# The first k and v loads of an attention and expert kernel: one GpSimd queue in order of use, instead of v beside k on the SyncE queue

## The chip, the cores and the metric

The kernel runs on one core of a Trainium2 chip. The metric is the time of one execution on the device, in microseconds (us); each kernel was run several times and the median is quoted, with the lowest and highest run. A run counts as slow here when it is over 1.5% above the fastest of its kernel; all runs were fast but two of one kernel near the end, which are left out there. A second kind of number comes from the trace of one profiled execution: times within it are counted from the start of its span, which is some 2 us shorter than the device time.

Four chips took part. The kernel before takes 315.7 us on the first, 320.5 on the second and third and 316.8 on the fourth (medians), so kernels are compared only with runs of the kernel before on the same chip. TensorE, VectorE, ScalarE, GpSimd and SyncE appear in the trace as PE (its weight loads as PEld), DVE, ACT, POOL and SP; a `q` after the name (SPq) is an engine's queue of issued transfers.

## The reference

```python
def phi(x):                                   # x is q or k, scaled by D ** -0.25
    h = einsum('bhsd,md->bhsm', x, omega) - sum(x * x, -1, keepdims=True) / 2
    return exp(h - max(h, -1, keepdims=True)) / sqrt(m)
q_p, k_p = phi(q_s), phi(k_s)
kv  = einsum('bhsm,bhsd->bhmd', k_p, v)
z   = sum(k_p, axis=2)
out = einsum('bhsm,bhmd->bhsd', q_p, kv) / (einsum('bhsm,bhm->bhs', q_p, z) + 1e-6)
# ... out becomes the tokens of a mixture of experts: one expert per token by argmax,
# or the expert of the token before where a local gate says so; relu(x @ w1[e]) @ w2[e] times p[e]
```

B = 8, H = 8, S = 576, head size 64, 128 features; 8 experts, 512 to 1024 to 512. Only the first steps matter here: k is projected by omega, the row maxima of the projection are taken, and exp(projection) is multiplied with v.

## The kernel before

The attention part works through 36 units of k (9 for each P = 0 to 3). Each runs through a chain: transposes on TensorE, a copy `kt` on VectorE, projections by `om_bd` on TensorE, row maxima `kmx` on VectorE, exponentials `kp` and `ek` on ScalarE, and `va` (v times ek) on GpSimd, which TensorE then multiplies with `kp`. The loads:

```python
def load(P, nm, g):
    # ... a tile for q, k or v: 8 rows of 9 * 64 for q, 4 for k and v; 1152 KB for q and v, 576 KB for k
    # k has 4 buffers (bf16, converted by the DMA), v has 3 (float32)
    cuts = [0, 4, 9] if (P, nm, g) == (0, "k", 0) else [0, 9]
    for c0, c1 in zip(cuts, cuts[1:]):
        c = slice(c0 * Dh, c1 * Dh)
        (nc.sync if nm == "v" else nc.gpsimd).dma_start(out=t_[:, :, c], in_=rows[nm][:, j0:j0 + nj, c])

load(0, "k", 0)
# ... om_f (omega) and wgf (gate weights) loaded from ScalarE
load(0, "v", 0)
load(0, "k", 1)
load(0, "v", 1)
```

Calls of one engine keep their order; calls of different engines don't wait for one another. "k0a" and "k0b" are below the two pieces of the first k tile (4 and 5 of 9 columns), "k1" the second k tile, "v0" and "v1" the v tiles of P = 0, and "v2" the first v tile of P = 1. What stands between the loads and the chain are some constants:

```python
make_identity(nc, ident)                       # GpSimd
# ... ident_bf, om2 on VectorE
nc.tensor.transpose(t_ps, om2.rearrange("p a d -> p (a d)"), ident_bf)
om_t2 = consts.tile([128, M], BF)
nc.vector.tensor_copy(om_t2, t_ps)             # from PSUM
nc.vector.memset(om_bd, 0.0)
nc.vector.tensor_copy(om_bd[0:64, 0:M], om_t2[0:64])      # from SBUF: called "the om_bd copy" below
nc.vector.tensor_copy(om_bd[64:128, M:], om_t2[64:128])
```

And the schedule of the later loads, by iteration of the main loop:

```python
at(-1, load, 1, "k", 0)
at(-1, load, 0, "q", 0)
for P in range(1, NP):
    # ...
    at(max(9 * P - 9, 2), load, P, "v", 0)
    at(9 * P - 10, load, P, "k", 1)
    at(9 * P - 4, load, P, "v", 1)
    at(9 * P + LAG - 11, load, P, "q", 0)
```

From about 130 us on the second part runs: "pages" of gathered tokens go through the experts, 38 of them, with TensorE full from about 160 us.

## Time and profile before

| | before |
|---|---|
| device time, median of 3 (lowest to highest) | 315.73 us (315.63 to 315.75) |
| span of the profiled run, and its own device time | 318.8 us, 320.79 us |
| mean granted TensorE clock of that run | 0.959 |
| DMA traffic | 60.22 MB in 51562 packets |
| row maxima of units 0, 1, 2, 3 start at | 15.36, 18.13, 19.60, 21.15 us |
| first transposes of q, first gather of tokens | 32.61, 135.31 us |

Note the second row: the run that was profiled took 5 us longer than the three that were timed. Its early part can be read by itself, but its whole span is no partner for another kernel's span. The lines that carry the reading are in the prediction. Three more of this trace are wanted below as landmarks; the first number is the start, the second the duration, and brackets hold the idle time ahead with what ended it:

```profile
21.15 1.22 DVE L200 TENSOR_REDUCE kmx<-pj 128x8 f32<-128x1024 f32 x1
...
32.61 0.41 PE L171 MATMUL tp<-ident_bf,arena 128*64 128x128 bf16 x8
...
135.31 1.09 POOL L574 DMA_INDIRECT xg<-x_tok,ix  x1 [5.45 <-DVE pe L508]
```

They mark the end of the start-up (unit 3's row maxima), the arrival of q in the chain, and the hand-over to the experts. An early gain is worth something only if it is still there at the third.

### The profile page before, as it was taken

The page shows a single profiled execution, that of the slowest core. Times are in us where ns is not written, and L with a number is a line of the kernel's source. Part 1 is how long each engine was busy: PE and PEld are TensorE (multiplying, and loading weights), DVE is VectorE, ACT ScalarE, POOL GpSimd, SP SyncE. Part 2 cuts the span into 40 slices and gives each one's busy share as a digit, 9 for nine tenths or more (in the row PEclk, how much of TensorE's full clock was granted, in tenths as well). Part 3 has the DMA queues.
Part 4 walks back from the last instruction along what each step waited for, and adds up shares of the span by engine and source line. Part 5 has one row for each costly group of instructions (what it writes and reads, how often), then busy time and mean ns, then how long its engine had stood idle before and what let it go on. Part 6 is the DMA issues. An engine that isn't in the chain of part 4 may idle for free. (4 is left out here: it accounts for less than half of the span.)

```text
span 318.8 us, 8136 instructions
## 1 busy us (share of the span) xinstructions
PE 257.5 (81%) x2977; PEld 153.7 (48%) x2977; DVE 179.9 (56%) x406; ACT 151.0 (47%) x228; POOL 175.1 (55%) x264
## 2 busy tenths in 40 slices
PE   0266778787877775737989989999999999999991
PEld 0154555565555653523656556644444444444440
DVE  3487578979879868953555674333333331433440
ACT  1057698988989877514455445512222121222000
POOL 8459845755477743186585632145536556533452
PEclk9999899999999979756999999999999999999998
DMA  7999999999979999969999953247656695842222
GB/s 246 291 208 262 293 210 283 248 238 241 288 128 222 228 237 226 227 178 199 196 216 223 226 129 72 51 120 192 173 143 159 171 179 138 168 143 94 103 118 88
DMA packets 51562, 60.22 MB, mean 189 GB/s; under 512 B 24464, under 2 KB 33680, under 8 KB 51520
## 3 DMA queue, kind: packets, MB, share of 16 engines
q0 software_dynamic: 23088, 40.58, 60.3%
q1 hardware_dynamic: 24352, 14.29, 17.0%
q10 hardware_dynamic: 4080, 4.77, 4.6%
q8 instruction: 28, 0.46, 0.6%
q14 instruction: 14, 0.11, 0.1%
HBM read 67.16 MB, written 14.68 MB: 257 GB/s over the span
## 5 line engine op out<-in xcount | busy, mean ns | idle before, releaser
L604 PE MATMUL pj<-w_all,xt 128*128 x304 | 76.4, 385 | 3.6 <-DVE lt L294 3.4
L609 ACT ACTIVATE arena<-pj 128x1024 bf16<-128x1024 f32 x38 | 38.9, 1023 | 75.5 <-PE pj L604 58.1
L635 POOL DMA_INDIRECT out_dram<-y,idr x38 | 37.8, 995 | 53.1 <-DVE y L634 39.0
L218 POOL TENSOR_TENSOR va<-vs,ek 128x512 bf16<-128x512 f32 (+1 forms) x40 | 38.1, 956 | 34.5 <-ACT ek L209 34.3
L574 POOL DMA_INDIRECT xg<-x_tok,ix x36 | 37.4, 1038 | 30.7 <-PE tp L587 12.5
L200 DVE TENSOR_REDUCE kmx<-pj 128x8 f32<-128x1024 f32 x36 | 44.0, 1221 | 13.5 <-ACT kvb L237 8.6
L206 ACT ACTIVATE kp<-pj 128x1024 bf16<-128x1024 f32 x36 | 37.4, 1040 | 18.9 <-DVE kmx L200 18.9
L143 POOL DMA_DIRECT2D w_all<-in_moe_w_dram x64 | 35.8, 564 | 16.7 <-DMA w_all<-in_moe_w_dram 11.8
L604 PEld LDWEIGHTS <-xt 128*128 128x128 bf16 x304 | 28.9, 99 | 31.8 <-ACT xt L589 3.0
L267 ACT ACTIVATE qp<-pj 128x1024 bf16<-128x1024 f32 x36 | 37.6, 1045 | 11.1 <-PE pj L261 5.9
L634 DVE TENSOR_SCALAR y<-po,prb 128x512 f32<-128x512 f32 x24 | 18.0, 751 | 34.0 <-PE po L629 19.6
L194 PE MATMUL pj<-om_bd,kt 128*128 128x256 bf16 x144 | 23.5, 288 | 2.9 <-ACT kp L206 1.3
L168 PE MATMUL tp<-ident_bf,ks 128*128 128x128 bf16 x128 | 13.3, 230 | 15.4 <-DMA ks<-in_k_dram 7.6
L291 DVE TENSOR_TENSOR xr<-po,rd 128x512 bf16<-128x512 f32 x36 | 24.9, 691 | 1.2
L619 DVE COPY ht<-tp 128x1024 bf16<-128x1024 bf16 (+1 forms) x20 | 12.2, 608 | 22.5 <-PE tp L616 18.6
L629 PE MATMUL po<-w_all,ht 128*128 x104 | 24.6, 379 | 0.2 <-DVE y L634 0.2
L589 ACT COPY xt<-tp 128x512 bf16<-128x512 bf16 x19 | 11.1, 584 | 25.3 <-PE tp L587 22.0
L629 PEld LDWEIGHTS <-ht 128*128 128x128 bf16 x160 | 15.2, 98 | 16.3 <-issue 0.3
L619 DVE COPY arena<-tp 128x512 bf16<-128x512 bf16 (+1 forms) x18 | 9.2, 513 | 24.5 <-PE tp L616 12.1
L716 ACT COPY qt<-tp 128x512 bf16<-128x512 bf16 x36 | 21.8, 605 | 1.2 <-DVE kt L714 1.0
L629 PE MATMUL po<-w_all,arena 128*128 x88 | 20.8, 379 | 1.6 <-DVE y L634 1.6
L629 PEld LDWEIGHTS <-arena 128*128 128x128 bf16 x144 | 13.8, 98 | 16.6 <-issue 1.7
(154 smaller groups left out, 374.9 us busy)
## 6 DMA issues: line engine op xcount, KB each, us to landing
w_all<-in_moe_w_dram POOLq DMA_DIRECT2D x64, 256.0 KB
vs<-in_v_dram SPq DMA_DIRECT2D x8, 1152.0 KB
arena<-in_q_dram POOLq DMA_DIRECT2D x4, 1152.0 KB
x_tok<-xr ACTq DMA_DIRECT2D x16, 256.0 KB
ks<-in_k_dram POOLq DMA_DIRECT2D x7, 576.0 KB
out_dram<-y,idr POOLq DMA_INDIRECT x38
xg<-x_tok,ix POOLq DMA_INDIRECT x36
x_tok<-xr ACTq DMA_DIRECT2D x4, 128.0 KB
```

The costliest lines, as they stand in the source:

```text
L143: nc.gpsimd.dma_start(out=wdst[l][:, ds(e * WE + i * 1024, 1024)].rearrange("p (c f) -> p c f", f=w), in_=src[e].rearrange(("(c p) f -> p ...
L194: nc.tensor.matmul(pj[:, 2 * i:2 * i + 2, :].rearrange("p a d -> p (a d)"), lhsT=kts[t][:, i], rhs=om_bd, start=True, stop=True)
L200: nc.vector.tensor_reduce(mx, kpj[t], axis=AX, op=Alu.max)
L206: nc.scalar.activation(kp, kpj.pop(t), Act.Exp, scale=scale)
L218: nc.gpsimd.tensor_tensor(va[:, x:x + 4 * n, 0:Dh].rearrange("p (h r) d -> p h r d", h=4), stg[P, "v", g].rearrange("p h (r d) -> p h r d" ...
L267: nc.scalar.activation(qp, qpj.pop(s), Act.Exp, scale=scale)
L291: nc.vector.tensor_tensor(xrs[s][:, u % 2, :].rearrange("p (g h d) -> p g h d", g=2, h=4), ov[:, :, :, 0:Dh], rd.to_broadcast([128, 2, 4, ...
L574: nc.gpsimd.indirect_dma_start(out=xg, out_offset=None, in_=src, in_offset=bass.IndirectOffsetOnAxis(ap=ix, axis=0), bounds_check=TE - 1, ...
L604: nc.tensor.matmul(h_ps[:, c, :], lhsT=xt[:, dc, :], rhs=w1_all[:, ds(ev + (dc * F + c * 512), 512)], start=(dc == 0), stop=(dc == DC - 1))
L609: nc.scalar.activation(h, h_ps.rearrange("p a x -> p (a x)").rearrange("p (c f) -> p f c", f=FC), Act.Relu)
L629: nc.tensor.matmul(y_ps[:, 0, :], lhsT=htn[0][:, f], rhs=w2_all[:, ds(ev + f * D, D)], start=(f == 0), stop=(f == FC - 1))
L635: s_ = nc.gpsimd.indirect_dma_start(out=out_flat, out_offset=bass.IndirectOffsetOnAxis(ap=idr[:, c:c + 1], axis=0), in_=y, in_offset=None, ...
```

## The change

Intent: k is what the chain needs first, yet v's large packets take turns with it. With the first k and v in one queue, in order of use, nothing should go ahead of the first k.

```diff
-            (nc.sync if nm == "v" else nc.gpsimd).dma_start(...)
+            (nc.sync if nm == "v" and P else nc.gpsimd).dma_start(...)
...
-    load(0, "k", 0)
+    for nm_, g_ in (("k", 0), ("v", 0), ("k", 1), ("v", 1)):
+        load(0, nm_, g_)
 # ... om_f, wgf from ScalarE as before
-    load(0, "v", 0)
-    load(0, "k", 1)
-    load(0, "v", 1)
```

From line 114 on, lines of the changed kernel have numbers lower by 2 (L200 becomes L198).

> **What bounds the kernel now.** The chain of work that ended last is of no use here: it holds two pieces at 313 us, 0.3% of the span. So I read in this order: the slices of the page, busy time by stage, the waits of the first 20 us against those after them, and then the first 20 us instruction by instruction. The slices:
>
> ```profile
> PE   0266778787877775737989989999999999999991
> DMA  7999999999979999969999953247656695842222
> ```
>
> A slice is 8 us. TensorE does nothing in the first and little in the second, while the DMA engines are at 90% or more from the second slice on. Three stages follow: a head in which compute waits for data, the attention part up to about 112 us with no engine full, and an expert part in which TensorE is full. Busy time by stage:
>
> ```profile
> core 0: us, PE busy (x) PEld busy (x) DVE busy (x) ACT busy (x) POOL busy (x), PEclk, DMA share, GB/s
> 0.00:17.00 17.00, 2.70 (x17) 1.75 (x18) 7.08 (x9) 1.67 (x2) 10.35 (x28) 1.00 0.98 265
> 17.00:112.00 95.00, 74.61 (x1543) 53.59 (x1540) 78.41 (x145) 81.26 (x142) 63.50 (x119) 0.98 1.10 238
> 112.00:160.00 48.00, 33.52 (x524) 22.18 (x523) 31.04 (x106) 24.20 (x37) 24.45 (x35) 0.79 1.00 211
> 160.00:220.00 60.00, 56.68 (x431) 33.26 (x429) 30.16 (x91) 27.48 (x34) 29.02 (x37) 1.00 0.69 151
> 220.00:313.00 93.00, 90.00 (x472) 42.88 (x470) 33.26 (x55) 16.37 (x16) 46.95 (x48) 1.00 0.56 147
> ```
>
> From 17 us on, ScalarE (81 of 95) and VectorE (78 of 95) alternate on a chain, and from 160 us TensorE sets the pace. Waits for a loaded tile lie in the head alone; over 20 to 112 us the longest wait for any DMA is 0.4 us, of a weight load's issue:
>
> ```profile
> PEld L168 <- DMA ks<-in_k_dram: 9.6, 2, 7.8
> PE tp L168 <- DMA ks<-in_k_dram: 7.6, 1, 7.6
> ...
> POOL w_all L143 <- DMA w_all<-in_moe_w_dram: 0.4, 1, 0.4
> ```
>
> So the change, which touches only loads of the head, can win only what the head loses. There, in order of time:
>
> ```profile
> 0.81 59.31 SPq L103 DMA_DIRECT2D vs<-in_v_dram  x7
> 1.35 2.49 POOL L103 DMA_DIRECT2D ks<-in_k_dram  x3 [0.84 <-POOLq L837]
> 5.60 4.07 DVE L130 COPY om_bd<-om_t 64x128 bf16<-64x128 bf16 x1
> 7.06 2.56 POOL L332 IOTA io<- 128x768 bf16 x1
> 12.76 0.61 PE L168 MATMUL tp<-ident_bf,ks 128*128 128x128 bf16 x4 [7.59 <-DMA ks<-in_k_dram]
> 16.63 0.61 PE L168 MATMUL tp<-ident_bf,ks 128*128 128x128 bf16 x4 [1.31 <-DVE kmx L200]
> 19.60 1.22 DVE L200 TENSOR_REDUCE kmx<-pj 128x8 f32<-128x1024 f32 x1
> ```
>
> Units 0 and 1 wait for the first piece of k until 12.76, unit 2 for the second until 16.63 (the weight load before it names that DMA, 1.79 us). VectorE's row maxima come at 15.36, 18.13, 19.60 and 21.15; from the third on they follow at about 1.5 us. Why k is late, in the queues from 6 to 15 us:
>
> ```profile
> q1 hardware_dynamic: 1004, 2.26, 71.2%
> q0 software_dynamic: 913, 0.51, 39.3%
> q10 hardware_dynamic: 965, 0.02, 6.2%
> ```
>
> q0 is GpSimd's queue (k and q), q1 SyncE's (v), q10 ScalarE's. They send nearly the same number of packets, so they take turns, but v's packets have 2304 bytes and k's here 512 or 640. SyncE has three v loads queued at once (v has three buffers), the third of which, P = 1, is used only some 30 us later.
>
> **What the Trainium skill says.** "DMA: Bandwidth & Descriptors", section "Queues, rings and completion order", says that each DMA engine goes round robin over the queues that have work, a packet at a time; the equal counts above agree. The same page, "Issuing engines are not separate DMA queues", says that the issuing engine does not choose other DMA engines: moving v between queues changes order and not bandwidth. The trace agrees: the engines stay full from 3 to 30 us whatever queue is sending. "SBUF — State Buffer", section "Who interferes with whom", says that VectorE's copies in a two-port mode and GpSimd exclude each other, and the later one blocks entirely. The trace agrees: the L130 copy lasts 4.07 us, its twin L131 0.20, and it ends at 9.67, just after GpSimd's IOTA (9.62). "TensorE: Matmul & The Clock Gate", "What's actually happening", says that TensorE is at half rate until a window of about 3.4 us was busy; here four projections take 1.06 us up to 19.4 and 0.60 from 20.46.
>
> **The change part by part.** *Order of the queues.* Before: SyncE v0, v1, v2 (v2 is the first v of P = 1), GpSimd k0a, k0b, k1, k2, q0, k3. The order of instructions after: GpSimd k0a, k0b, v0, k1, v1, then the constants, then k2, q0, k3; SyncE has six v loads left, and its first, v2, now goes out at once, at 0.81. It finds the engines empty, as GpSimd's first packet came only at 6.0 (issue 1.35, so 4.7 us later). v2 thus takes the place of v0, 2.2 to about 6, and costs k nothing; v1 alone moves behind k1, v0 behind k0b.
>
> *When data land.* One load is 512 packets. Alone, v sends 350 packets in the 2 us from 3.75, so 512 take 2.9 us. 1152-byte packets (2397 in 13 us, 16 to 29) take 2.8 us a load. A 512-byte packet takes 59 ns in the trace and a 640-byte one 67, so over 16 engines k0a is 1.9 us and k0b 2.1, with 0.3 us each for ScalarE's small packets in turn. Summed from 6.0, with 0.3 for v2's tail: k0a sent by 8.5, k0b 10.9, v0 13.8, k1 16.6, v1 19.5, k2 22.3, q0 28.0, k3 30.8. Add 0.6 to 0.9 for the slowest engine and the signal (k1 in before: first of the 16 signals at 18.5, last at 19.4). k0a lands near 9.2 instead of 12.7, k0b at 11.6 instead of 16.6, k1 near 17.2 instead of 19.4.
>
> *What is added.* Two more issues on GpSimd ahead of the identity: 2 x 0.8 (2.49 for three) = 1.6 us. The identity, IOTA and the rest move by that: IOTA ends at 11.3. If the om_bd copy stays blocked until then, both om_bd copies end at 11.5, and only then comes the first kt copy (13.40 in before). So k's first 3.5 us are not all used: 13.40 - 11.5 = 1.9 us for unit 0.
>
> *The chain from there*, with durations of before, TensorE cold: kt0 11.5 to 11.9; second transposes 12.0; projections of unit 0 12.4 to 13.4; row maxima 0 13.45 to 14.7 (1.23), kt2 to 15.1, row maxima 1 15.1 to 16.3, kt3 to 16.75, row maxima 2 16.85 to 18.1, kt4, row maxima 3 18.5. In before that last one began at 21.15. Gain: 21.15 - 18.5 = 2.6 us. From the second gate: the transposes of unit 4 need k1, near 17.2; they are followed by the projections of unit 3 (0.6 + 0.6), and maxima 3 at 18.5 again. Both gates give the same 2.6, which is why I trust it. v0 lands at 14.5, its first use (after 16) is later.
>
> *What carries on.* k2 is needed near 26, lands at 23; q0 lands near 28.8, needed at 32.61 - 2.6 = 30.0; v1 lands at 20.3, needed near 23.5. Later loads have 8 us or more of slack by their landing times. The DMA engines must also follow 2.6 us earlier. They are full for most of 2 to 138 us, but have free time at 88 to 96 (share 0.77, 131 GB/s) and a little at 60 to 66; I estimate 4 to 5 us of it, more than 2.6. So the first gather, at 135.31 now, which waits for VectorE there, should move too, and the TensorE-bound rest with it. I take off 0.2 for small collisions: 315.73 - 2.4 = 313.3.
>
> **The rivals.**
> (1) The om_bd copy is the new gate and is blocked even longer by the extra GpSimd work: one more us lost, gain 1.5, about 314.2. For it: the 4.07 us. Against: it ended with IOTA, and the same list of work follows it.
> (2) q0 or k1 are late: the v load of P = 1, second half, goes out on SyncE 2.6 us earlier and takes turns with q0. Then iteration 9 stalls by 1 to 1.5 us: about 314.5. Against: in before that v load was issued at 27 and sent almost nothing until GpSimd's backlog ended at 29.75.
> (3) All is hidden: the weight loads fill the DMA engines, so the expert part begins when it did, 315.7. For it: GpSimd's weight loads at 112 to 130 wait for earlier ones, 0.4 to 1.4 us each. Against: the free time before 96 us, and that the gathers then wait 5.45 us for VectorE, not for a DMA.
> (4) The clock: TensorE has half its clock in several windows of 3.4 us between 115 and 150 (mean 0.79 from 112 to 160). One window more or fewer is up to 1.7 us of full-rate work, in either direction. I cannot predict it.
> (5) A larger gain: om_bd is not blocked, and k0b at 11.6 is the gate. But k1 caps it: again about 2.6.
>
> **Range and chances.** The middle is 313.3. Rivals 1 to 3 make it 314 to 315.7, a clock window fewer 311.6, so 311.5 to 315.9 holds 8 times in 10. Over 2% would be 309.4 or 322.0: the whole gap from 9.9 to 12.76 and the second stall together are not 6.3 us, so faster is 0.03; slower needs a large new stall, 0.02; within 2% is 0.95.
>
> **What would show it.** First transposes of k near 9.3 and not 12.76, but the first kt copy only near 11.5, with a long om_bd copy before it ending with IOTA; row maxima 3 near 18.5; no wait of GpSimd's va products for v; the first transposes of q near 30; first gather near 132.7. Queue q1 holding one v load in the first 15 us. It would be wrong if the first gather is still at 135 (rival 3), if the transposes of q wait for the DMA (rival 2), or if the head gains 2.6 and the end shows something else with another mean clock (rival 4).

## The result, and the profile after

| | before | after |
|---|---|---|
| median (lowest to highest), 4 runs each, alternating on one chip | 315.74 us (315.63 to 315.86) | 314.27 us (313.95 to 315.04) |
| ratio, with 95% interval | | 0.9957 (0.9939 to 0.9975) |
| row maxima of unit 3 | 21.15 us | 18.35 us |
| first transposes of q | 32.61 us | 29.80 us |
| first gather | 135.31 us | 132.77 us |

A ratio is the mean time of one kernel's fast runs over that of the other's of the same rounds, so it is not quite the ratio of the medians quoted. The change gains 1.4 us (0.4%): faster beyond doubt, the same within 2%. The head, instruction by instruction, in the trace of the changed kernel:

```profile
0.81 30.52 SPq L103 DMA_DIRECT2D vs<-in_v_dram  x3
1.35 1.75 POOL L103 DMA_DIRECT2D ks<-in_k_dram  x2 [0.84 <-POOLq L835]
...
7.11 4.07 DVE L128 COPY om_bd<-om_t 64x128 bf16<-64x128 bf16 x1
8.56 0.61 PE L166 MATMUL tp<-ident_bf,ks 128*128 128x128 bf16 x4 [1.88 <-DMA ks<-in_k_dram]
8.57 2.56 POOL L330 IOTA io<- 128x768 bf16 x1
11.43 0.42 DVE L712 COPY kt<-tp 128x512 bf16<-128x512 bf16 x1
11.91 0.59 PE L166 MATMUL tp<-ident_bf,ks 128*128 128x128 bf16 x4 [2.74 <-DVE kt L712]
...
16.66 0.64 PE L169 MATMUL tp<-ident_bf,ks 128*64 128x128 bf16 x8
...
18.35 1.22 DVE L198 TENSOR_REDUCE kmx<-pj 128x8 f32<-128x1024 f32 x1
...
29.80 0.41 PE L169 MATMUL tp<-ident_bf,arena 128*64 128x128 bf16 x8
...
132.77 1.09 POOL L572 DMA_INDIRECT xg<-x_tok,ix  x1 [4.08 <-DVE pe L506]
```

k is there at 8.56, and TensorE transposes it at once. Then TensorE stands still for 2.74 us for a `kt` copy, and that copy waits behind the long om_bd copy, which began at 7.11 and ended at 11.18, just after GpSimd's IOTA (8.57 + 2.56 = 11.13). So the wait for k has become a wait for VectorE. The queues from 6 to 15 us, to be laid beside those in the prediction (packets, MB, share):

```profile
q0 software_dynamic: 1768, 2.29, 114.5%
q10 hardware_dynamic: 552, 0.00, 5.8%
q1 hardware_dynamic: 1, 0.00, 0.0%
```

SyncE's queue, which had sent 1004 packets of v in this time, sends one. GpSimd's queue goes from 0.51 to 2.29 MB. The slices of the changed kernel:

```profile
PE   0487778787877865838989989999999999999990
PEclk9999799989999999556999999999999999999998
```

TensorE gets from 2 to 4 tenths in the second slice of 8 us. In PEclk, 7, 8, 5, 5 and 6 are slices in which TensorE ran partly at half its clock (9 is 90% or more). The kernel before has such places too, in other slices:

```profile
PEclk9999899999999979756999999999999999999998
```

The same by stage, to be laid beside the table of stages in the prediction (columns as there):

```profile
0.00:17.00 17.00, 5.48 (x37) 3.71 (x37) 9.10 (x13) 3.30 (x4) 13.01 (x32) 1.00 1.00 254
17.00:112.00 95.00, 75.28 (x1552) 53.68 (x1548) 77.44 (x146) 81.30 (x144) 62.63 (x118) 0.96 1.11 242
```

In the first 17 us TensorE is busy 5.48 us instead of 2.70: work of the chain has moved into them. The clock of the second stage is 0.96 instead of 0.98. In the trace that is two windows of 3.4 us at half clock, at 34.0 and 61.3 us, instead of one at 36.9. (The trace's clock record begins at about 20 us only. For the time before, the column says 1.00, though four projections take 1.06 us there and 0.60 later.)

Two questions stand. Why is the head's gain 2.8 us and not more, when k itself came 4.2 us earlier (12.76 to 8.56)? And why does the time gain only 1.4 us of a head that gains twice that?

### The profile page after: what moved, and what is told of

It reads as the page before. It is cut to its first block, busy times and chain, and to the rows that moved or that the text cites. A ratio compares the mean times of both kernels' runs of the same rounds, so it can differ in the third digit from the quotient of the medians.

```text
span 313.1 us, 8136 instructions
## 1 busy us (share of the span) xinstructions
PE 259.5 (83%) x2977; PEld 154.4 (49%) x2977; DVE 180.2 (58%) x406; ACT 151.3 (48%) x228; POOL 176.7 (56%) x266
## 5 line engine op out<-in xcount | busy, mean ns | idle before, releaser
L198 DVE TENSOR_REDUCE kmx<-pj 128x8 f32<-128x1024 f32 x36 | 43.9, 1220 | 14.4 <-PE pj L192 6.6
L141 POOL DMA_DIRECT2D w_all<-in_moe_w_dram x64 | 35.8, 564 | 17.2 <-DMA w_all<-in_moe_w_dram 11.6
L602 PEld LDWEIGHTS <-xt 128*128 128x128 bf16 x304 | 28.8, 99 | 29.7 <-issue 1.7
L265 ACT ACTIVATE qp<-pj 128x1024 bf16<-128x1024 f32 x36 | 37.6, 1044 | 11.3 <-PE pj L259 11.3
L192 PE MATMUL pj<-om_bd,kt 128*128 128x256 bf16 x144 | 24.7, 300 | 2.3 <-ACT qp L265 0.7
## 6 DMA issues: line engine op xcount, KB each, us to landing
w_all<-in_moe_w_dram POOLq DMA_DIRECT2D x64, 256.0 KB, 11.3
vs<-in_v_dram SPq DMA_DIRECT2D x6, 1152.0 KB, 11.3
```

The costliest lines, as they stand in the source:

```text
L141: nc.gpsimd.dma_start(out=wdst[l][:, ds(e * WE + i * 1024, 1024)].rearrange("p (c f) -> p c f", f=w), in_=src[e].rearrange(("(c p) f -> p ...
L192: nc.tensor.matmul(pj[:, 2 * i:2 * i + 2, :].rearrange("p a d -> p (a d)"), lhsT=kts[t][:, i], rhs=om_bd, start=True, stop=True)
L198: nc.vector.tensor_reduce(mx, kpj[t], axis=AX, op=Alu.max)
L265: nc.scalar.activation(qp, qpj.pop(s), Act.Exp, scale=scale)
L602: nc.tensor.matmul(h_ps[:, c, :], lhsT=xt[:, dc, :], rhs=w1_all[:, ds(ev + (dc * F + c * 512), 512)], start=(dc == 0), stop=(dc == DC - 1))
```

## The experiments

My theory had two parts. First: the bytes that go ahead of k decide when k comes, the blocked om_bd copy then decides when the chain starts, and k1 sits close behind. Second: the lead is carried to the end, and what is missing in the time lies in half-clock windows of TensorE. The rivals: that k1 alone is the gate; that it matters that there is one queue; that the expert part gives the lead back because a DMA bounds it.

### The two kernels again

Both kernels were run once more, unedited, on a second chip, with profiles, to have a pair of traces from one chip. (The times expected here and below were those of the first chip.)

> The kernel before itself, for a second profile and more times. The one profile of before was of a run of 320.8 us, 5 us over its timed median, so it is no fair partner for the end of the span. Theory (extra half-clock windows ate part of the head's gain): time 315.7 within 0.3, row maxima of unit 3 again at 21.1 to 21.2 us, and a number of half-clock windows of TensorE that differs from profile to profile. Rival (the loss is a new stall of the changed kernel at 61 to 66 us, whatever the clock): this run shows nothing at 61 to 66, and the changed kernel's second profile shows the stall again at the same place.

> The changed kernel itself, second profile. Its first profile led before by 2.7 us from 20 to 61 us, then by 1.68 after a half-clock window at 61.3 to 64.7 us. Theory (clock): time 314.0 to 314.7, head again 2.7 to 2.9 us ahead of before, and the window at 61 us somewhere else or absent, so that the lead at 90 us is either 2.7 or again reduced by about 1 us for each window. Rival (a stall of its own): the lead drops at 61 to 66 us again, with full clock.

Medians: before 320.49 us (11 runs; the kernel submitted as a repeat 320.12, ratio 0.998, interval 0.9938 to 1.0023), after 318.67 (ratio 0.9955, interval 0.9916 to 0.9995). The repeat shows how wide the noise is on this chip: runs of the kernel before differ by 3.5 us here, by 0.2 on the first chip. The gain of the change comes out as on the first chip. In the traces unit 3's row maxima start at 20.96 and 18.36, so the head gains 2.60 us; the first gathers come at 135.29 and 132.50, a lead of 2.79; the relu of page 27 at 246.28 and 243.28, a lead of 3.0; the spans end at 318.79 and 316.86, a lead of 1.93. So in this pair the lead of the head is all there until 243 us, and 1.1 us of it go in the last 70 us. They don't go in half-clock windows. About 0.5 us go between pages 27 and 29 (leads of 3.00 and 2.46), at a clock of 1.00: TensorE waits there 0.80 us for VectorE's `y`, against 0.28 at the same place in the kernel before, and not for a DMA. The other 0.5 us go after GpSimd's last store to the output was issued (313.06 and 310.59, still a lead of 2.47), when TensorE has no work left.

A closer look at how a lead is lost: the lead of the first pair of traces, taken instruction by instruction, is constant at 2.70 us from 44 to 61 us, falls to 1.68 across 61.3 to 64.7 us, and is constant again to 112 us (at the first gather it is 2.54 again). At that place the changed kernel's TensorE is at half clock. Busy time before and in the window (columns as in the stages; the fourth number from the end is POOL, then clock, DMA share, GB/s):

```profile
57.80:61.30 3.50, 2.18 (x57) 1.48 (x55) 3.33 (x8) 3.09 (x6) 2.72 (x5) 1.00 1.11 258
61.30:64.70 3.40, 3.40 (x80) 2.34 (x74) 0.77 (x1) 1.37 (x4) 1.73 (x3) 0.50 1.10 299
```

The same two stretches in the repeat of the same kernel:

```profile
57.80:61.30 3.50, 2.18 (x61) 1.53 (x60) 3.27 (x7) 3.10 (x6) 2.67 (x5) 1.00 1.11 255
61.30:64.70 3.40, 3.33 (x106) 2.63 (x98) 1.82 (x3) 2.47 (x5) 1.73 (x3) 1.00 1.10 302
```

Same kernel, same TensorE work ahead (2.18 of 3.50 us busy), and once the clock is 0.50 for 3.4 us and once it is not. Unit 19's row maxima come at 58.67 in the first and 58.62 in the second, unit 20's at 63.93 and 62.84: this one window costs 1.0 us. The kernel before has the same accident at 63.9 us in its repeat and not in its first trace. So a window moves a lead by about a microsecond in either direction, and a pair of traces or two are too few to say where the lead goes in general.

### k1 ahead of v0

The order k0, k1, v0, v1 in the same queue. If k1 had a part in the 18.35, this moves it.

```diff
-    for nm_, g_ in (("k", 0), ("v", 0), ("k", 1), ("v", 1)):
+    for nm_, g_ in (("k", 0), ("k", 1), ("v", 0), ("v", 1)):
```

> One queue, but both halves of k ahead of both of v, so k1 lands 2.8 us earlier, near 13.4 instead of 16.1. If the gate of the head is the blocked om_bd copy and the chain from it (my theory), the row maxima of unit 3 stay at 18.35 within 0.2 and the time stays within 0.4 of the changed kernel. If k1 is the gate (the rival I named as second), they come earlier, up to 0.5 to 2 us, and the time falls by as much.

Measured: unit 3's row maxima at 18.36 us, unchanged; median 318.64 us, ratio 0.9959 (0.990 to 1.0018), as the changed kernel.

So k1 is not the gate in the changed kernel. There the last of k1's 16 signals came at 16.1 us, and unit 4's transposes at 16.66 name no wait for it.

### The om_bd copy taken away from SBUF

The two copies read the transposed omega where TensorE left it, in PSUM, instead of its copy in SBUF. This is the changed kernel with one edit:

```diff
-    nc.vector.tensor_copy(om_bd[0:64, 0:M], om_t2[0:64])
-    nc.vector.tensor_copy(om_bd[64:128, M:], om_t2[64:128])
+    nc.vector.tensor_copy(om_bd[0:64, 0:M], t_ps[0:64])
+    nc.vector.tensor_copy(om_bd[64:128, M:], t_ps[64:128])
```

> The two om_bd copies read the transposed omega out of PSUM and not out of SBUF, [...]about 0.2 us each, done near 7.5 instead of 11.4. Theory: the first kt copy comes at 9.2 instead of 11.4 (k0a is there at 8.56), units 0 and 1 run 2 us earlier, but unit 4's transposes then wait for k1 at 16.1, so the row maxima of unit 3 come only 0.3 to 0.6 earlier (17.8 to 18.1) and the time by as much. Rival (another thing holds that copy): it stays 4 us long and nothing moves.

In its trace:

```profile
7.11 0.22 DVE L128 COPY om_bd<-tp 64x128 bf16<-64x128 bf16 x1
...
16.18 0.30 PE L169 MATMUL tp<-ident_bf,ks 128*64 128x128 bf16 x4 [1.34 <-DMA ks<-in_k_dram]
...
17.12 1.23 DVE L198 TENSOR_REDUCE kmx<-pj 128x8 f32<-128x1024 f32 x1 [0.17 <-PE pj L192]
...
29.71 0.41 PE L169 MATMUL tp<-ident_bf,arena 128*64 128x128 bf16 x8 [0.60 <-DMA arena<-in_q_dram]
```

The copy that took 4.07 us takes 0.22, at the same place beside the same GpSimd work, so the 4.07 was blocking and not work. The first row maxima come at 11.36 instead of 13.39 (2.0 us earlier), and unit 3's at 17.12 (1.25 earlier; I had expected less). Now unit 4's transposes wait 1.34 us for k1: k1 is the next gate, but it stands 1.25 us further on and not at the same place. And at 29.71 q is late by 0.60: SyncE's v load, issued earlier like all the rest, takes turns with q (286 packets of v from 26 to 30 us, against 179 in the changed kernel). Of the 1.25 us there are 0.76 left at unit 9. The median is 317.93 us, ratio 0.9931 (0.9888 to 0.9974).

### Both edits

k1 ahead of v0, and the om_bd copies from PSUM.

> Both gates at once: k0a, k0b, k1, v0, v1 in the one queue, and om_bd out of PSUM. Theory: row maxima of unit 3 near 16.2 instead of 18.35, 2.1 us more than the changed kernel; v0 lands near 16, later than its scale, so GpSimd's products start late and may give back up to 0.8; q lands near 27.4 and is needed near 27.7. Time 1.3 to 2.2 below the changed kernel, 312.2 to 313.0. If the head's gain does not carry to the end (rival 3 of the prediction, all hidden behind the weight loads), the time stays near 314.2 although the head is 2 us shorter.

Unit 3's row maxima come at 15.96 (2.4 us before the changed kernel's), but unit 9's at 29.15, only 0.6 before its 29.74. In between:

```profile
16.28 1.05 POOL L216 TENSOR_TENSOR va<-vs,ek 128x512 bf16<-128x512 f32 x1 [2.93 <-DMA vs<-in_v_dram]
...
24.40 0.30 PE L232 MATMUL po<-va,kp 64*128 64x65 bf16 x8 [2.29 <-POOL va L220]
...
25.34 1.23 DVE L198 TENSOR_REDUCE kmx<-pj 128x8 f32<-128x1024 f32 x1 [3.29 <-ACT kvb L235]
```

v0 now lands at about 16.1, GpSimd waits 2.93 us for it, TensorE waits 2.29 for GpSimd's va, and the row maxima wait 3.29 for the copy `kvb` of what TensorE made of it. I had allowed 0.8 us of give-back; it was about 1.8 (2.4 less 0.6). Median 318.94 us against 320.53 on this third chip, ratio 0.9936 (0.9882 to 0.9989). I had expected 1.3 to 2.2 us below the changed kernel; the gain over the kernel before is 1.8 us here (means), where that of the changed kernel was 1.3 to 1.5 on its chip, so most of it is not seen, though the intervals overlap. With k, v0 and the constants all close behind one another, taking away one wait uncovers the next.

### The kernel before with only v2 out of the way

The rival "it matters that there is one queue" says that v on SyncE beside k is the trouble. This is the kernel before, in which v0 and v1 stay on SyncE and only v2 goes to GpSimd's queue, behind q:

```diff
-(nc.sync if nm == "v" else nc.gpsimd).dma_start(...)
+(nc.sync if nm == "v" and (P, g) != (1, 0) else nc.gpsimd).dma_start(...)
```

> The kernel before with one load moved: only the third v load (first half of v of P = 1) goes from SyncE to GpSimd's queue, behind q; v0 and v1 stay on SyncE beside k. Theory (what hurt was the number of bytes ahead of k, not the queue that they are in): v0 alone from 2.2 to 6, then v1 in turns with k0a until about 11, k0b and k1 alone: k0b lands near 13.7, k1 near 16.6, row maxima of unit 3 near 18.8, 2.3 us earlier than before; time 314.3 to 314.8. Rival (v beside k in another queue is the harm, as the change has it): hardly any gain, row maxima 3 after 20, time over 315.2.

```profile
11.31 0.61 PE L168 MATMUL tp<-ident_bf,ks 128*128 128x128 bf16 x4 [6.14 <-DMA ks<-in_k_dram]
...
18.40 1.23 DVE L200 TENSOR_REDUCE kmx<-pj 128x8 f32<-128x1024 f32 x1
```

k comes at 11.31, far later than the changed kernel's 8.56, yet unit 3's row maxima come at 18.40 against 18.35: in the changed kernel the blocked copy eats that difference. The time is 318.74 us, ratio 0.9921 (0.9868 to 0.9974), no worse than the change itself. At unit 9 this version is 1.1 us behind the changed kernel (30.84 and 29.74), at unit 20 only 0.25 (63.09, and 62.84 in that kernel's second trace). So moving one tile, 1152 KB that nothing needs for 30 us, does all that the change does for unit 3 and no less for the time.

### One queue, wrong order

The changed kernel with v0 and v1 ahead of k.

```diff
-    for nm_, g_ in (("k", 0), ("v", 0), ("k", 1), ("v", 1)):
+    for nm_, g_ in (("v", 0), ("v", 1), ("k", 0), ("k", 1)):
```

> The changed kernel with the order in the one queue reversed: v0, v1, then k0a, k0b, k1. Theory (order counts, not the queue): k0a lands near 14.4, k0b 16.4, k1 19.2; row maxima of unit 3 near 21.8, 0.6 later than before and 3.4 later than the changed kernel; time 315.8 to 317. Rival (one queue by itself helps, by sparing the engines the turns between queues): it stays below 315.2.

Unit 3's row maxima come at 22.04 us, as expected, 1.1 later than the repeat of the kernel before. The time is 323.71 us against 320.53, ratio 1.0094 (1.0033 to 1.0155): slower by 3 us where the head explains 1.1. This is a miss in size. Its runs were at half clock for 35.5 us on average against 29.8 for the kernel before on the same chip, which by the fit below is 0.8 us more; the rest of some 1 us is not explained. But its direction settles the rival: one queue by itself gains nothing, the order does.

### Both kernels without the expert part

To see whether the missing 1.4 us is given back in the expert part, both kernels were cut off after the attention and routing parts. They give a wrong result on purpose.

```diff
-        if 0 in lists and not pages:
+        if False:
...
-    wload = [(l, e, i) for l in range(2) for e in range(E) for i in range(4)]
+    wload = [(l, e, i) for l in range(1) for e in range(E) for i in range(4)]
...
+    # zeros to out[0:128], then return, ahead of the loop over pages
```

> The kernel before without its expert part (wrong result on purpose: no pages, no second set of weights, one block of zeros written), so that the time ends with the attention part and without the late waits of the last pages. Time 135 to 150 us, the partner of the next two runs.

> The changed kernel with the same cut. Theory (the head's 2.6 us carry through the attention part, and what is missing at the end, 2.6 against about 1.4, is lost to half-clock windows and to the last pages): median 2.2 to 2.9 us under the cut kernel before. Rival (part of the gain is given back inside the attention part, by the weight loads or the stores): 1.0 to 1.8 us under it.

| cut off | runs | mean us | mean us at half clock |
|---|---|---|---|
| before | 5 | 154.59 | 28.8 |
| after | 5 | 153.17 | 36.1 |
| best version (below), fast runs of 6 | 4 | 151.16 | 31.2 |

Time at half clock is worked out from each run's span and mean granted clock as 2 x span x (1 - clock). Without any pages the means differ by 1.41 us, with a standard error of 0.55 worked out from the ten runs; the medians, 154.35 and 153.68, differ by 0.67. I had expected 2.2 to 2.9. The result lies in the range that I had given to the rival, that part of the gain is lost inside the attention part, but with this error it doesn't rule out the whole 2.6. So a shortfall seems to appear without any page; these runs don't measure it well. In the profiles of these two, unit 3's row maxima lead by 3.16 us (21.36 and 18.20), unit 35's by 3.38 (109.72 and 106.34), and the ends by 2.06 (152.30 and 150.24). Followed instruction by instruction, the lead falls from 3.39 to 2.17 us between 110 and 124 us. There the changed kernel's clock is 0.77, 0.84 and 0.70 (stretches of 5 us from 110 on), and that of the kernel before 1.00. So in this pair the loss does lie at half clock.

The last column says the same of the runs. A least-squares fit over these 14 fast runs, with one constant for each kernel, gives 0.16 us (standard error 0.03) of time for each microsecond at half clock. At equal time at half clock the changed kernel would be 2.6 us faster (standard error 0.3), which is the gain of the head. The 7.4 us more at half clock are 7.4 x 0.16 = 1.2 us. This is a correlation over few runs, worked out after the fact, and the half-clock time in it includes stretches in which TensorE has nothing to do; no run took the half clock away. It points at the windows, it doesn't prove them. The same fit over the 76 runs of the full kernels on the second to fourth chip, with a constant for each chip, gives 0.14 us (standard error 0.02) for each microsecond at half clock, and the changed kernel 1.94 us faster (standard error 0.45) at equal half clock, against 1.3 us as measured. There the runs at half clock are 30.9 us for the changed kernel and 26.3 for the one before (means, second chip). So in the full kernel the windows would stand for 0.6 us, and another 0.7 of the head's 2.6 would be missing without them, though that is little more than the standard error.

Whether an early start itself brings more half clock, I can't say. The changed kernel has more of it in both comparisons, full and cut; but the version with v first starts later and also has more, and the one with v2 moved starts 2.6 us earlier and has less (27.4 against 29.8).

### A version that takes the three waits together

The experiments name three waits: for k behind v2's bytes, for the blocked om_bd copy, and for v0 when k1 goes ahead of it. So: v0 goes out alone on SyncE, where it is nearly done by the time GpSimd's first packets go, at about 6 us; k0, k1, v1 and q follow in GpSimd's queue; v2 goes behind q; and om_bd is copied from PSUM.

```diff
 # against the kernel before
-(nc.sync if nm == "v" else nc.gpsimd).dma_start(...)
+(nc.sync if nm == "v" and (P, g) not in ((0, 1), (1, 0)) else nc.gpsimd).dma_start(...)
-    load(0, "k", 0)        # and the three other loads further down
+    for nm_, g_ in (("k", 0), ("v", 0), ("k", 1), ("v", 1)):
+        load(0, nm_, g_)
-        at(max(9 * P - 9, 2), load, P, "v", 0)
+        at(9 * P - 9 if P > 1 else -1, load, P, "v", 0)
+# om_bd copied from t_ps, as above
```

> A version meant to beat both: om_bd out of PSUM; v0 on SyncE, alone, in the time before GpSimd's first packet; GpSimd k0a, k0b, k1, v1, then k2, q, v2, k3. k1 lands near 13.5 and v0 near 6.5, so neither unit 4 nor the va products wait. Row maxima of unit 3 near 16.0 (18.35 in the changed kernel), first q transposes near 27.4 (29.8), no DMA wait there as q lands near 25.5. If the head's gain carries: 4 to 5 us under the kernel before, ratio 0.984 to 0.989. Rival (what the earlier head gains is lost again to clock and tail): ratio 0.992 or more, like all the others so far.

> The same version with the cut. Theory: 4.4 to 5.4 us under the cut kernel before, about twice the changed kernel's gain. Rival (the weight loads bound the attention part): no more than 3 us under it.

```profile
7.89 0.61 PE L166 MATMUL tp<-ident_bf,ks 128*128 128x128 bf16 x4 [1.96 <-DMA ks<-in_k_dram]
...
14.97 1.22 DVE L198 TENSOR_REDUCE kmx<-pj 128x8 f32<-128x1024 f32 x1
...
29.61 1.04 POOL L216 TENSOR_TENSOR va<-vs,ek 128x512 bf16<-128x512 f32 x1 [1.17 <-DMA vs<-in_v_dram]
...
35.69 0.40 PE L169 MATMUL tp<-ident_bf,ks 128*64 128x128 bf16 x4 [2.94 <-DMA ks<-in_k_dram]
```

The head is 6.0 us earlier than that of the kernel before (20.96), 3.4 earlier than the changed kernel's, with no wait for q or k1, and at unit 9 all of it is still there (26.38, against 32.55 in the first trace of the kernel before). At unit 20 the lead over that trace is 3.7 us (61.90 and 65.61), and so it is at unit 35 (105.75 and 109.49). Unit 9's va waited 1.17 us for v2, the price of sending it late. The 2.4 us given back between units 9 and 20 go at 35.69, where TensorE has waited 2.94 us for k3, the second k tile of P = 1: the lead over that trace is 6.9 us at unit 11 and 3.2 at unit 12. In this version k3 is issued at 7.54, behind v2 (6.78) in the same queue, and lands 28.1 us later. So v2 again goes ahead of a k tile that is needed sooner. No run tried the two the other way round. The result is correct, the median 312.51 us against 316.75 on the fourth chip, ratio 0.9863 (0.9832 to 0.9893): 1.4% faster, the best version of the study. The 4.1 us (means) agree with the lead at unit 35 and not with that of the head. Cut off without the expert part its four fast runs gain 3.4 us (means, the table above; 2.8 with the two slow ones); I had expected 4.4 to 5.4, so that was a miss.

## Why the prediction was right

The predicted time was 313.3 us, in a range of 311.5 to 315.9; the measured 314.27 lies in it, 1 us above the middle, and "within 2%" came true. The range also held 315.7, no gain at all, so that the time lies in it proves little; the landmarks of the trace prove more. Step by step:

- **Order of the queues: right.** Queue q1 sent one packet from 6 to 15 us; v2 went first and cost k nothing. GpSimd's first packets again came late, at 5.8 us (put at 6.0, and at 5.8 in the kernel before too).
- **When k lands: 0.7 us too late.** The first transposes ran at 8.56, predicted 9.2 to 9.3. The first piece was sent by 8.2 (put at 8.5), and TensorE began 0.4 us after that, where I had added 0.6 to 0.9 for the slowest engine and the signal. It did not matter, since the next step was the gate.
- **The om_bd copy is blocked until IOTA ends: right.** Predicted IOTA end 11.3 and kt copy 11.5; measured 11.13 and 11.43. The experiment with PSUM shows the cause: the copy falls to 0.22 us and the chain starts 2.0 us earlier.
- **The chain from there: right.** Unit 3's row maxima predicted at 18.5, measured at 18.35. The gain was put at 2.6; it is 2.80 in the first pair of traces and 2.60 in the second.
- **"Both gates give the same 2.6, which is why I trust it": wrong.** The second gate, k1, was put at 17.2; the last signal was at 16.1, and sending k1 earlier changed nothing. The number was right for one reason, not for two.
- **What carries on: right up to the first gather.** q at 29.80 (predicted 30.0), first gather at 132.77 (predicted 132.7). How close the second is owes something to luck: in between, a window took the lead down to 1.68 us, and it came back.
- **The sum: 2.4 predicted, 1.4 measured.** The mis-sized term is the last, "0.2 for small collisions": in its place some 1.2 us of the 2.6 are missing. The prediction had listed half-clock windows as rival 4, "one window more or fewer is up to 1.7 us", without giving them a share of the middle. What it named as their sign came in part: the head gained 2.6 to 2.8 and the end showed 1.4; the clocks of the first chip's timed runs of the kernel before are not on record. One window in the attention part cost 1.0 us, where the same stretch was seen with it and without. How much of the 1.2 us the windows took stays open: the fit gives them all of it in the cut kernels and 0.6 us in the full ones, and in the pair of full traces from one chip the last 1.1 us went at full clock or after TensorE's last work.

The rivals: (1) a longer blocked copy did not happen. (2) A late q did not happen in the changed kernel, but it did, with 0.60 us, as soon as the chain came another 1.25 us earlier. (3) The weight loads did not hide the gain: the first gather moved with the head. (4) The clock is where a part of the missing time points. (5) "om_bd not blocked, k1 caps it: again about 2.6" fell: without the block the head gained another 1.25 us.

## What to carry to other kernels

When queues are sending at once, count the bytes that go ahead of the transfer that gates, whatever their queue, and move those that nothing needs soon; one tile of 1152 KB was the whole effect here, and putting all into one queue gained nothing by itself. Then look at what the moved transfer now goes ahead of: in the best version it cost 2.94 us at the next k tile. Before counting on an earlier arrival, ask what else the first consumer waits for: a small copy blocked behind another engine's work held back 2 us of it, and reading from another memory took the block away. Measure a gain of a microsecond or two against the run-to-run changes of the clock, with repeats on one chip, as one window at half clock is worth as much.

## What the Trainium skill lacked or had wrong

- "DMA: Bandwidth & Descriptors", section "Specifications", gives about 1 us from issue to the first byte for GpSimd's queue. At the start of this kernel the first packets came at 5.8 us after an issue at 1.35, some 4.4 us later, in the kernel before and in the changed one.
- "TensorE: Matmul & The Clock Gate", section "What's actually happening": its table of two states has half rate follow after an idle window of about 3.4 us. The length agrees, but that rule alone doesn't foretell the windows here: one at 0.50 followed on 3.50 us in which TensorE was busy for 2.18, and in a second run the same work was followed by none. One such window cost 1.0 us in this kernel's attention part.
- "SBUF — State Buffer", section "Who interferes with whom", has VectorE's copy and GpSimd's instruction exclude each other for one instruction, by who issues first. Here a 64 x 128 copy of 0.22 us lasted 4.07 us, 7.11 to 11.18, though the IOTA that it ended with began only at 8.57: it stayed blocked over several GpSimd instructions in a row. With its source in PSUM it was free of it at the same place (0.22 us). The trace shows these times, not who held the ports.
- "DMA: Bandwidth & Descriptors", section "Queues, rings and completion order": that queues take turns packet by packet agrees (1004, 913 and 965 packets), and what follows from it, that the queue with the larger packets gets most of the bytes, is what made k late (2.26 MB of v and 0.51 MB of k). The page doesn't draw the conclusion.
